# Head of a delta-rule attention and GELU layer kernel: chunks 2 and 3 loaded early, unread products among the row steps, one back turn as ScalarE copies

## The chip, the cores and the metric

The kernel runs on one core of one Trainium2 chip. The metric is the device time of one execution in microseconds, as the median of several runs. One further execution was taken by the hardware profiler, and all views below come from it.

## The reference

Two layers run one after the other. The first is a delta-rule attention with 4 batches, 8 heads, 768 tokens and a head dimension of 48; the second is a layer of 384 -> 2048 -> 384 with an exact GELU over the 3072 tokens that come out of the first.

```
k_n = k / (norm(k) + 1e-6)
for t in range(768):
    y[:, :, t] = q_t @ state
    v_old      = state^T k_n_t
    state      = state + beta_t * outer(k_n_t, v_t - v_old)
x = y.transpose(0, 2, 1, 3).reshape(3072, 384)
h = x @ w_in;  g = 0.5 * h * (1 + erf(h / sqrt(2)));  out = g @ w_out
```

`q`, `k`, `v` and `beta` are 32-bit floats. `w_in` and `w_out` are 64-bit floats: the kernel reads them as pairs of 32-bit words and makes 32-bit floats of them with integer and float operations.

## The kernel before

**Units and chunks.** The 768 tokens are cut into 12 chunks of 64. A unit is one chunk of one pair of batches (one batch in partitions 0 to 63, the other in 64 to 127), so that each chunk has two units (`a` = 0, 1). `first` are the four units of chunks 0 and 1, `third` those of chunk 2, `fourth` those of chunk 3. Two chunks form a group of 32 small triangular systems, which are solved together.

**The head**, the part that the change is about, is written out by hand (L1201 to L1299) in a fixed order on all engines and on the DMA queue SP. In it:

- K and Q of the units are turned on TensorE (`transposed`, L405, part 0 is K and part 1 is Q) and copied out by ScalarE; `grams` (L445) multiplies K by K, `queries` (L463) K by Q.
- `eliminate_steps(0)` (L491) yields the steps that invert the 32x32 triangles of group 0: `scales`, `flip`, thirty row steps `eliminate(j)`, j = 1 to 30 (L528 a product into `tmp`, L530 an addition into `Nu`, both on VectorE), `diagonal`, then three back turns `back(0)` to `back(2)`. A back turn is a VectorE transpose of the whole `Nu`: the first into `XM` (L539), the second into the right half of `Zf`, the third into the left half (both L543). `clear` then sets the lower rows of the left half to zero, mostly on GpSimd (L560).
- `join` (L568) makes the 64x64 inverse of two 32x32 ones at two levels: products on TensorE (`psJ`, L578), at level 0 a VectorE product into `XM` (L589), at level 1 a copy into `Zf` (L593).
- `solve` (`psU`, L792), `use` and `read` (`psY`, L822), `update` (`psS`, L834) and `turn` (`psX`, `xT`, L883) take the two units of chunk 0 to the input of the second layer.

**The weights** come in 16 parts: parts 0 to 7 are `w_in`, 8 to 15 are `w_out`. `fetch(n)` (L234) loads part n from the queue SP, `begin` (L252, or L255 where there is one kink), `exponents` (L258, ScalarE), `mantissas` (L272, L274) and `signed` (L281, L282) decode it. Parts for which `two_kinks(n)` holds have two ScalarE operations in `exponents` and no L281 in `signed`; the others have one ScalarE operation and L281. There are four raw buffers for `w_in`, so that `signed(n)` issues `fetch(n + 4)`, which waits for the last reader of the raw words of part n: L281, or L274 where there is no L281.

**The rest** is a list of steps with due times (`at(first, last, steps)`, from L1316), sorted by time and traced in that order. VectorE and GpSimd run them in just this order; for TensorE, ScalarE and SP a planner takes, at each moment of its own model, the earliest traced instruction that it thinks ready. Instructions that are given to `keep` stay in the traced order on ScalarE. `fc1` (L915) makes the hidden layer of chunks 0 and 1 (16 blocks `f` for each, two to a part of `w_in`), with a GELU into `G` after each block, `fc2` (L933) the output. `load(3)` has 12 DMA issues, `load_v(2)` 4. The tile `G` holds the GELU's results and is idle in the head.

```
def fetch_in(dst, src, u, queues=(nc.sync, nc.sync)):
    ...
    for p in range(2):
        queues[p].dma_start(out=dst[HALF[p]],
```

Of the kernel before, what the change touches and what calls it, by code (L numbers as in the profile page):

```python
# [19 lines left out]
def kernel(  # L20
# [28 lines left out]
    nc = tc.nc  # L49
# [136 lines left out]
    G = Gp[0]  # L186
    spare = Gp[1].rearrange("q a f n -> q (a f n)")
# [51 lines left out]
    def two_kinks(n):  # L239

        return 2 < n < n_in or n_in + 3 < n < n_in + 7
# [27 lines left out]
    def mantissas(n):  # L269
        dst, lo, hi, e = halves[n]  # L270
        bits = dst.bitcast(U32)
        nc.vector.tensor_scalar(bits, hi, 0xFFFFF, 0x100000, op0=ALU.bitwise_and,  # L272
                                op1=ALU.bitwise_or)
        nc.vector.scalar_tensor_tensor(dst, lo, 2.0 ** -32, bits, ALU.mult, ALU.add)  # L274
# [24 lines left out]
    def decode_in():  # L299

        marks = {3: (None, 1.05, 0.99, 1.06), 4: (1.0, 1.09, 1.1, 1.13),
                 5: (1.12, 1.18, 1.14, 1.2), 6: (1.19, 1.24, 1.21, 1.25),
                 7: (1.245, 1.3, 1.29, 1.36)}
        steps = []
        for n, (a, b, c, d) in marks.items():
            if a is not None:
                steps += [(a, (begin, n))]
            steps += [(b, (exponents, n, keep)), (c, (mantissas, n)), (d, (signed, n))]
        return steps
# [95 lines left out]
    def transposed(u, part=(0, 1)):  # L405
        for x in part:
# [10 lines left out]
            flat = (Qp[2 + u.a] if u.c == 3 and x == 0 else (u.Kp, u.Qp)[x]).rearrange("q h d -> q (h d)")  # L417
# [73 lines left out]
    def eliminate_steps(g):  # L491
# [44 lines left out]
        def back(x):  # L536
            nu = Nus[g]
            if x == 0:
                nc.vector.transpose(XMs[g].rearrange("q u c -> q c u"),  # L539
                                    nu.rearrange("q i c -> q c i"))  # L540
            elif x == 1 or g == 0:
                cols = slice(HB, C) if x == 1 else slice(0, HB)
                nc.vector.transpose(Zf[g % 2][:, :, cols].rearrange("q u i -> q i u"), nu)  # L543
            else:
                for p in range(2):
                    top = slice(p * C, p * C + HB)
                    if g > 2:
                        nc.gpsimd.tensor_copy(Zf[0][top, :, 0:HB], Zf[0][top, :, HB:C])
                    else:
                        nc.scalar.copy(Zf[0][top, :, 0:HB], Zf[0][top, :, HB:C])  # L550

        def clear(g):
                for cc in range(2):
                    for p in range(2):
                        part = Zf[g % 2][p * C + HB:(p + 1) * C,
                                         cc * NU // 2:(cc + 1) * NU // 2, 0:HB]
                        if g == cc == p == 0:
                            nc.scalar.mul(part, low[0:HB, 0:HB // 2], 0.0)
                        else:
                            nc.gpsimd.memset(part, 0.0)  # L560

# [3 lines left out]
        steps += [(1.9, back, x) for x in range(3)]  # L565
        return steps + [(0.0, clear, 0)] if g == 0 else steps
# [342 lines left out]
    def fc1(c, f):  # L909
# [8 lines left out]
        if c == 0 or f < EARLY:  # L918
            keep(nc.scalar.activation, *gelu)
        else:  # L920
            nc.scalar.activation(*gelu)  # L921
# [270 lines left out]
    def signs(c0, c1):  # L1192
# [11 lines left out]
        mybir.EngineType.PE, mybir.EngineType.SP}))  # L1204
    load_v(0)
    for n in range(2):
        fetch(n)
    load_k(2, "Kp")
# [13 lines left out]
    scales_, flip_, *rows, back0, back1, back2, clear_ = [s_[1:] for s_ in eliminate_steps(0)]  # L1222
    factors(gms[0], beta_m[:, 0:2].rearrange("q c a h -> q (c a) h"), n0)
    scales_[0]()
    flip_[0]()
# [3 lines left out]
    signs(2, NC)  # L1229
    third = [tiles[2, a] for a in range(NA)]  # L1230
    sums_ = [(u, h) for u in third for h in range(H)]
    for u in first:
        transposed(u, (1,))
        if u.c == 1:
            for x in sums_[5 * u.a:5 * u.a + 5]:
                sum_of_squares(*x)
        queries([u])
    for a in range(NA):
        fetch_q(tiles[2, a])
    for a in range(NA):  # L1240
        fetch_in(Qp[2 + a][:, :, 0:D], k, tiles[3, a])
    for n in range(2, NS):
        fetch(n)
    for n in range(n_in, n_in + 3):
        fetch(n)
    load_v(1)
    for u in third:
        transposed(u, (0,))
    for x in sums_[10:13]:
        sum_of_squares(*x)  # L1250
    grams(third)
    for u in third:
        transposed(u, (1,))
    for x in sums_[13:]:
        sum_of_squares(*x)
    fourth = [tiles[3, a] for a in range(NA)]
    for u in fourth:
        transposed(u, (0,))
    grams(fourth)
    for fn, *args in rows:  # L1260
        fn(*args)
    nc.vector.scalar_tensor_tensor(ng, gms[0][:, 0:NA], -1.0, ns[0], ALU.mult, ALU.mult)
    back0[0](*back0[1:])
    against_state(first[:NA])
    for u in first:
        masked(u)
    back1[0](*back1[1:])
    for a in range(NA):
        join(0, (a,), 0)
    back2[0](*back2[1:])  # L1270
    for a in range(NA):
        join(0, (a,), 1)
    clear_[0](*clear_[1:])
    for u in first[NA:]:
        scale_v(u)
    begin(0)
    exponents(0)
    mantissas(0)
# [30 lines left out]
    def state_at(c, *times, first=(), second=(), last=()):  # L1309

        steps = state_steps(c, first, second, last)
        if len(times) > len(steps):
# [8 lines left out]
             [(t, (join, 0, range(NA, 2 * NA), level)) for level, t in enumerate((1.085, 1.16))],  # L1321
# [24 lines left out]
    plan += [at(2.22, 2.44, [(1.0, scale_head, tiles[c, a], h)  # L1346
# [125 lines left out]
```

## Time and profile before

| quantity | value |
| --- | --- |
| median of 3 runs | 626.86 us (626.41 to 626.89) |
| the profiled execution | 626.5 us, span 624.7 us |
| mean granted TensorE clock | 0.985 |
| TensorE matmul busy | 604.7 us (97%) |
| VectorE busy | 440.4 us (70%) |
| ScalarE busy | 240.5 us (39%) |
| GpSimd busy | 212.8 us (34%) |
| chain that ended last | TensorE 88%, VectorE 5%, ScalarE 3%, DMA 2%, issue 1% |

The span runs from the first to the last instruction; 1.8 us of the profiled execution lie outside it. In the 40 slices of the page, TensorE is busy for 6 to 8 tenths in the first three slices (15.6 us each) and for 9 tenths in nearly all that follow; the granted clock reads 9, 9, 7, 6 in the first four slices and 9 after them. VectorE is busy for 7 to 9 tenths in the first nine slices. A TensorE product of 32-bit floats counts as two instructions (the 64 products of each `fc2` chunk pair are listed as 128), a transpose as one.

### The profile page before, as it was taken

How to read it: one execution, taken by the hardware profiler on the slowest of the kernel's cores; microseconds unless marked ns; L12 is line 12 of the kernel's file. 1: busy time of each engine (PE TensorE's matmuls, PEld its weight loads, DVE VectorE, ACT ScalarE, POOL GpSimd, SP SyncE). 2: the span in 40 equal slices, each digit the busy share in tenths (PEclk: the TensorE clock that was granted, in tenths of full speed). 3: DMA queues.
4: the chain of work that ended last, by engine and by line, in shares of the span. 5: the costliest groups of instructions: out<-in, count | busy, mean ns of one | idle time of the engine just before them, and what ended most of it. 6: DMA issues, size and time to landing. Idle time of an engine off the chain costs nothing.

```text
span 624.7 us, 19703 instructions
## 1 busy us (share of the span) xinstructions
PE 604.7 (97%) x8358; PEld 539.8 (86%) x8358; DVE 440.4 (70%) x811; ACT 240.5 (39%) x546; POOL 212.8 (34%) x316
## 2 busy tenths in 40 slices
PE   6789999999999999999999999999999999999997
PEld 5578786676799999998899998899998899988997
DVE  7999899988967697774859755859745947332532
ACT  3576876265443165224451134451134222044200
POOL 4045002000369821687222885222885200000000
PEclk9976999999999999999999999999999999999999
DMA  9686775101433452353123533013421001010011
GB/s 130 162 269 164 168 185 136 25 1 37 72 41 50 76 92 39 56 115 39 16 44 54 92 73 38 13 31 55 75 50 17 12 3 27 4 24 1 0 27 26
DMA packets 159576, 39.64 MB, mean 63 GB/s; under 512 B 151168, under 2 KB 154368, under 8 KB 159488
## 3 DMA queue, kind: packets, MB, share of 16 engines
q1 hardware_dynamic: 156816, 37.34, 30.7%
q10 hardware_dynamic: 2672, 1.03, 0.8%
q8 instruction: 66, 1.08, 0.7%
q14 instruction: 22, 0.18, 0.1%
HBM read 33.62 MB, written 4.72 MB: 61 GB/s over the span
## 4 chain that ended last, share of the span: by engine, by line
PE 88%; DVE 5%; ACT 3%; DMA 2%; issue 1%; SPq 0%; ACTq 0%
PE psX L966 13%; PE psY L1032 11%; PE psY L966 9%; PE psX L1032 8%; PE psZ L1032 6%; PE psV L1032 6%; PE psH L915 5%; PE psO L933 4%; PE psZ L966 4%; PE psV L966 4%; PE psG L440 3%; PE psK L732 3%; PE psY L822 2%; PE psU L792 2%; PE psQ L752 2%; PE psT L419 2%
## 5 line engine op out<-in xcount | busy, mean ns | idle before, releaser
L377 POOL TENSOR_TENSOR n<-n,half 128x16 f32<-128x16 f32 x10 | 30.8, 3079 | 178.8 <-DVE n L375 131.0
L530 POOL TENSOR_TENSOR Nu<-Nu,tmp 128x30 f32<-128x30 f32 (+14 forms) x120 | 65.3, 544 | 9.4
L528 POOL TENSOR_TENSOR tmp<-Nu 128x30 f32<-128x30 f32 (+14 forms) x120 | 62.5, 520 | 9.4
L1032 PE MATMUL psX<-xT,w_in_sb 128*128 128x256 f32 (+1 forms) x288 | 62.6, 346 | 0.0
L966 PE MATMUL psX<-w_out_sb,G 128*128 128x192 f32 x320 | 56.1, 329 | 0.0
L966 PEld LDWEIGHTS psX<-w_out_sb,G 128*128 128x128 f32 x320 | 52.2, 190 | 0.7
L1032 PEld LDWEIGHTS psX<-xT,w_in_sb 128*128 128x128 f32 x288 | 47.9, 190 | 5.4
L915 PE MATMUL psH<-xT,w_in_sb 128*128 128x256 f32 x192 | 44.6, 386 | 2.3 <-ACT G L921 1.1
L915 PEld LDWEIGHTS psH<-xT,w_in_sb 128*128 128x128 f32 x192 | 36.0, 191 | 9.6 <-ACT G L1015 2.5
L933 PE MATMUL psO<-w_out_sb,G 128*128 128x384 f32 x128 | 43.9, 490 | 0.0
L851 DVE TENSOR_TENSOR V<-psY,y 64x192 f32<-64x192 f32 (+1 forms) x60 | 21.3, 356 | 30.4 <-PE psY L834 26.4
L1060 DVE TENSOR_TENSOR psY<-psY,pu 128x512 f32<-128x512 f32 x20 | 14.0, 700 | 40.3 <-PE psY L1032 40.3
L1032 PE MATMUL psY<-xT,w_in_sb 128*128 128x256 f32 (+1 forms) x192 | 41.5, 345 | 0.0
L1015 ACT COPY xT<-psX 128x768 f32<-128x768 f32 x9 | 7.2, 800 | 79.8 <-PE psX L892 79.8
L1015 ACT COPY pu<-psZ 128x512 f32<-128x512 f32 x40 | 23.5, 587 | 37.5 <-PE psZ L1032 35.0
L933 PEld LDWEIGHTS psO<-w_out_sb,G 128*128 128x128 f32 x128 | 23.5, 190 | 14.2 <-issue 0.3
L1032 PEld LDWEIGHTS psY<-xT,w_in_sb 128*128 128x128 f32 x192 | 32.1, 191 | 3.5
L1015 ACT ACTIVATE G<-G 128x512 f32<-128x512 f32 x40 | 25.2, 631 | 21.2 <-DVE G L1068 21.0
L1068 DVE TENSOR_TENSOR G<-psY,pu 128x512 f32<-128x512 f32 x20 | 13.8, 690 | 22.2 <-PE psY L1032 21.5
L1015 ACT ACTIVATE G<-psY 128x512 f32<-128x512 f32 x20 | 11.9, 596 | 45.2 <-PE psY L1032 45.2
L966 PE MATMUL psY<-w_out_sb,G 128*128 128x192 f32 x160 | 28.1, 329 | 0.0
L966 PE MATMUL psZ<-T,pu 128*128 128x192 f32 x160 | 28.1, 329 | 0.0
(208 smaller groups left out, 1376.2 us busy)
## 6 DMA issues: line engine op xcount, KB each, us to landing
Kp<-in_k_dram SPq DMA_DIRECT2D x76, 96.0 KB, 3.2
w_out_sb<-in_moe_w_in_dram SPq DMA_DIRECT2D x24, 256.0 KB, 4.4
V<-in_v_dram SPq DMA_DIRECT2D x48, 96.0 KB, 3.1
w_raw<-in_moe_w_out_dram SPq DMA_DIRECT2D x12, 384.0 KB, 4.4
out_dram<-o_sb SPq DMA_DIRECT2D x40, 96.0 KB, 2.2
Qp<-in_k_dram SPq DMA_DIRECT2D x64, 32.0 KB, 2.2
G<-in_moe_w_out_dram SPq DMA_DIRECT2D x4, 384.0 KB, 5.1
Qp<-in_q_dram SPq DMA_DIRECT2D x96, 16.0 KB, 2.0
```

Source lines behind the costliest of these rows:

```text
L377: nc.gpsimd.tensor_tensor(flat, flat, half, op=ALU.pow)
L440: nc.tensor.matmul(psG[HALF[p], r, i * NP + j, :], lhsT=u.Kt[rows, p, j, :], rhs=(u.Qt if x else u.Kt)[rows, p, j, :], start=True, stop=True)
L528: rows_on.tensor_tensor(tmp, nu[:, j + 1:, j:j + 1].to_broadcast([128, n, j]), nu[:, j:j + 1, 0:j].to_broadcast([128, n, j]), op=ALU.mult)
L530: rows_on.tensor_tensor(nu[:, j + 1:, 0:j], nu[:, j + 1:, 0:j], tmp, op=ALU.add)
L732: nc.tensor.matmul(u.psK[HALF[p], r, j, :], lhsT=u.Kt[rows, p, j, :], rhs=SQ[rows, u.a, p ^ r, j, 0:w], start=True, stop=True)
L851: nc.vector.tensor_tensor(dst, src, pairs(u.y[at_], s), op=ALU.add)
L915: nc.tensor.matmul(psH, lhsT=w_in_sb[:, f // 2, m, f % 2 * 128:(f % 2 + 1) * 128], rhs=xTs[c][:, m, :], start=(m == 0), stop=(m == NM - 1))
L933: nc.tensor.matmul(u.psO, lhsT=G[:, u.a, f, :], rhs=w_out_sb[:, f, :], start=(f == 0), stop=(f == NF - 1))
L966: nc.tensor.matmul(ps_, lhsT=lhs[:, f, :], rhs=rhs[:, f, :], start=first and f == 0, stop=f == FH - 1, skip_group_check=not first)
L1015: i = fn(*args, **kw)
L1032: nc.tensor.matmul(ps_[:, i], lhsT=lhs[:, f // 2, f % 2 * 128:(f % 2 + 1) * 128], rhs=rhs, start=first and i == 0, stop=True, skip_group_c ...
L1060: nc.vector.tensor_tensor(L1["Y1"], L1["Y1"], L1["pu"][:, 0], op=ALU.add)
```

## The change

What it does, by parts:

1. `Q` of chunk 2 and `K` of chunk 3 get places in the tile `G` (`early_q`, `early_k`, their padding set to zero by four more GpSimd memsets), and their loads, with `K` of chunk 2, are issued ahead of `load_v(0)` and of the first weights. `load_v(1)` and `fetch(2)`, `fetch(3)` follow directly.
2. The turns and products of chunks 2 and 3 (`turned`, `grams`) move from before the row steps to between them: each is tied by a wait to the row step that was traced last (`behind_rows`). Between the others come 59 products of 128 columns that nobody reads (`unread`): 43 behind rows 13 to 30, 10 behind the last row and 6 behind the joins of level 0.
3. The third back turn goes. The left half of `Zf` is filled by ScalarE copies of the right half (`upper_left`), for chunk 0 in the head and for chunk 1 later; its lower rows are set to zero early by two GpSimd memsets.
4. `begin(0)` and half of `mantissas(0)` stand between the joins of level 1, and the second of these is copied out by VectorE. Part 2 of `w_in` becomes one with two kinks.
5. `fetch` of parts 8, 9 and 10 leaves the head for time 1.1, behind `load(3)`, `load_v(2)` and `signed(3)`, whose time goes from 1.06 to 1.081.
6. All GELUs of `fc1` are kept in order on ScalarE, and `scale_head` of chunks 2 and 3 moves from 2.22 to 2.125.

```
+    early_q, early_k = [[G[:, a, 4 * i:4 * i + 4].rearrange("q f (e n) -> q (f e) n", n=C)
+                         for a in range(NA)] for i in range(2)]
+    for a in range(NA):
+        tiles[2, a].Qp = early_q[a]
+        for x in (early_q, early_k):
+            nc.gpsimd.memset(x[a][:, :, D:], 0.0)
...
-        return 2 < n < n_in or n_in + 3 < n < n_in + 7
+        return 1 < n < n_in or n_in + 3 < n < n_in + 7
...
-        marks = {3: (None, 1.05, 0.99, 1.06), 4: (1.0, 1.09, 1.1, 1.13),
+        marks = {3: (None, 1.08, 0.99, 1.081), 4: (1.0, 1.112, 1.1, 1.13),
...
-            elif x == 1 or g == 0:
-                cols = slice(HB, C) if x == 1 else slice(0, HB)
-                nc.vector.transpose(Zf[g % 2][:, :, cols].rearrange("q u i -> q i u"), nu)
+            elif x == 1:
+                nc.vector.transpose(Zf[g % 2][:, :, HB:C].rearrange("q u i -> q i u"), nu)
...
+    def upper_left(us, put=lambda fn, *args: fn(*args)):
+
+        for p in range(2):
+            top = slice(p * C, p * C + HB)
+            put(nc.scalar.copy, Zf[0][top, us, 0:HB], Zf[0][top, us, HB:C])
...
-        if c == 0 or f < EARLY:
-            keep(nc.scalar.activation, *gelu)
-        else:
-            nc.scalar.activation(*gelu)
+        keep(nc.scalar.activation, *gelu)
...
+    load_k(2, "Kp")
+    for a in range(NA):
+        fetch_q(tiles[2, a])
+    for a in range(NA):
+        fetch_in(early_k[a][:, :, 0:D], k, tiles[3, a])
     load_v(0)
     for n in range(2):
         fetch(n)
-    load_k(2, "Kp")
+    load_v(1)
+    for n in range(2, NS):
+        fetch(n)
...
     scales_[0]()
+    for p in range(2):
+        nc.gpsimd.memset(Zf[0][p * C + HB:(p + 1) * C, :, 0:HB], 0.0)
     flip_[0]()
...
+    def behind_rows(fn, *args):
+
+        after = latest(mybir.EngineType.DVE)
+        n = len(nc.cur_bb.bb.instructions)
+        fn(*args)
+        new = next(i for i in nc.cur_bb.bb.instructions[n:] if i.engine == mybir.EngineType.PE)
+        tc.add_manual_dep(new, after.name,
+                          mybir.DependencyInfo(mybir.DependencyClass.Sync,
+                                               mybir.DependencyReason.DATA), reason="time")
+
+    def unread(*cols):
+
+        psI = ps.tile([128, 512], F32, tag="mlp", name="psI")
+        for n in cols:
+            nc.tensor.matmul(psI[:, 0:n], lhsT=ident,
+                             rhs=Kp[0].rearrange("q h d -> q (h d)")[:, 0:n], start=True, stop=True)
...
+    between = {12: [(turned, third, 0)], 13: [(unread, *[128] * 5)], 14: [(grams, third)],
+               15: [(turned, third, 1)], 16: [(unread, *[128] * 5)], 17: [(turned, fourth, 0)],
+               18: [(unread, *[128] * 4)], 19: [(grams, fourth)]}
+    between.update({j: [(unread, *[128] * 3)] for j in range(20, 26)})
+    between.update({j: [(unread, 128, 128)] for j in range(26, HB - 1)})
+    between[25] = [(unread, *[128] * 4)]
     for fn, *args in rows:
         fn(*args)
+        for step in between.get(args[0], ()) if args else ():
+            behind_rows(*step)
...
     nc.vector.scalar_tensor_tensor(ng, gms[0][:, 0:NA], -1.0, ns[0], ALU.mult, ALU.mult)
+    behind_rows(unread, *[128] * 10)
     back0[0](*back0[1:])
-    against_state(first[:NA])
-    for u in first:
+    against_state(first[:1])
+    for u in first[:3]:
         masked(u)
+    against_state(first[1:NA])
+    masked(first[3])
     back1[0](*back1[1:])
+    upper_left(slice(0, NA * H))
     for a in range(NA):
         join(0, (a,), 0)
-    back2[0](*back2[1:])
-    for a in range(NA):
-        join(0, (a,), 1)
-    clear_[0](*clear_[1:])
+    unread(*[128] * 6)
+    begin(0)
+    join(0, (0,), 1)
+    exponents(0)
+    mantissas(0, (0,))
+    join(0, (1,), 1, nc.vector.tensor_copy)
+    mantissas(0, (1,))
     for u in first[NA:]:
         scale_v(u)
-    begin(0)
-    exponents(0)
-    mantissas(0)
...
+             at(1.05, 1.051, [(1.0, upper_left, slice(NA * H, NU), keep)]),
+             at(1.1, 1.102, [(1.0, fetch, n_in + i) for i in range(3)]),
...
-    plan += [at(2.22, 2.44, [(1.0, scale_head, tiles[c, a], h)
+    plan += [at(2.125, 2.35, [(1.0, scale_head, tiles[c, a], h)
```

## The prediction

> **What bounds the kernel now.** I read the busy times by stretches first, then the chain of waits, then the timelines of VectorE and of the queue SP. From 67 us on TensorE hardly pauses, so the end moves as far as the work ahead of it does. In the chain, VectorE carries the head: rows, back turns, joins, decoding.
>
> The stretches (us, busy time and instructions of PE, PEld, DVE, ACT, POOL; then the granted clock):
>
> ```profile
> 36.00:37.00 1.00, 0.69 (x5) 0.45 (x3) 0.91 (x3) 0.96 (x3) 0.00 (x0) 1.00 0.79 264
> 37.00:38.00 1.00, 0.00 (x0) 0.00 (x0) 0.89 (x4) 0.98 (x2) 0.00 (x0) 1.00 0.68 176
> 39.00:40.00 1.00, 0.38 (x7) 0.14 (x5) 1.00 (x3) 1.00 (x7) 0.89 (x2) 0.80 0.95 330
> 40.00:41.00 1.00, 1.00 (x37) 1.00 (x40) 1.00 (x1) 0.41 (x1) 1.00 (x2) 0.50 1.02 269
> 56.00:57.00 1.00, 1.00 (x7) 0.87 (x4) 1.00 (x2) 0.40 (x1) 1.00 (x1) 0.66 0.06 16
> ```
>
> After a nearly idle stretch on TensorE the clock halves near 39.6 (0.80 in that stretch), and it comes back only at 56.7, when the first full products of the layer run; VectorE stands at 0.9 to 1.0 throughout. VectorE's timeline:
>
> ```profile
> 44.27 0.86 DVE L589 TENSOR_TENSOR XM<-psJ,gm 32x256 f32<-32x256 f32 x2 [0.39 <-PE psJ L578]
> 45.16 1.93 DVE L543 STREAM_TRANSPOSE Zf<-Nu 128x1024 f32<-128x1024 f32 x1
> 46.93 0.55 DVE L255 TENSOR_SCALAR w_e<-w_out_sb 128x768 uint32<-128x768 uint32 x1
> 47.39 0.97 DVE L272 TENSOR_SCALAR w_in_sb<-w_out_sb 128x768 uint32<-128x768 uint32 x1
> 52.19 1.47 DVE L282 SCALAR_TENSOR_TENSOR w_in_sb<-w_in_sb,w_e 128x768 f32<-128x768 f32 x1
> 53.69 1.07 DVE L255 TENSOR_SCALAR w_e<-w_out_sb 128x768 uint32<-128x768 uint32 x1
> 59.07 0.95 DVE L281 SCALAR_TENSOR_TENSOR w_e<-w_out_sb,w_e 128x768 uint32<-128x768 uint32 x1
> 77.28 1.02 DVE L765 TENSOR_TENSOR V<-psK,V 128x384 f32<-128x384 f32 x2 [0.75 <-ACT y L756]
> ```
>
> The third back turn, the wait of 0.39 ahead of the joins and three operations longer than their like (0.97, 1.47 and 1.07 against 0.55, 0.96 and 0.55) are in line. The queue SP (start, us to issue):
>
> ```profile
> 52.18 9.15 SPq L234 DMA_DIRECT2D w_out_sb<-in_moe_w_in_dram  x9
> 61.46 1.28 SPq L100 DMA_DIRECT2D Kp<-in_k_dram  x2
> 62.98 2.44 SPq L234 DMA_DIRECT2D w_out_sb<-in_moe_w_in_dram  x3
> 65.47 2.59 SPq L119 DMA_DIRECT2D Qp<-in_q_dram  x4
> 68.17 1.28 SPq L100 DMA_DIRECT2D Kp<-in_k_dram  x2
> 69.50 2.62 SPq L119 DMA_DIRECT2D Qp<-in_q_dram  x4
> 72.22 3.35 SPq L100 DMA_DIRECT2D V<-in_v_dram  x4
> ```
>
> SP issues without a break from 61.5 to 76: two K loads of `load(3)`, then part 7 of `w_in` as soon as its buffer is free (62.98), then the rest of `load(3)` and `load_v(2)`. The earliest traced ready DMA goes first.
>
> **Part by part**, against the profiled 626.5 us (span 624.7 and 1.8 outside; 0.36 under the median, to which I add the result).
>
> Early loads: 4 K, 8 Q and 4 K issues move ahead of V and weights. At their rates now (3.98, 7.26, 2.65 us) they end near 26; V of chunk 0 follows to 30, parts 0 and 1 to 33, V of chunk 1 to 38, parts 2 and 3 to 42. With some 5 us to land, V is there by 34 (wanted 39.1), part 0 by 38 (wanted 45), part 2 by 46 (wanted 54). K of chunk 3 lands near 29 for row 17 at 29.1; late, it would hold only TensorE. Cost nothing; the cover is 5 us.
>
> Row steps: they stay at 0.22 to 0.41 us each on VectorE and end at 38.9. Two memsets of 32x1024 on GpSimd now lie at 16 to 19 beside them. The row of such a memset beside L272 shows 0.42 lost, beside the following L274 (two inputs, 0.96) nothing; I take 0, with 0.4 as the far end. [...]
>
> Unread products: 59, two instructions each. The same shape, `psX` L879, runs two in 0.22 us, so 13 us of TensorE in time that waits for rows. The ten behind row 30 take 2.2 us and end at 41.2, just when the first back turn delivers `XM`. At half clock it is 4.4 us. I take the full clock, since no gap over 0.5 us is left between rows 12 and 30; the other end is a rival.
>
> VectorE, 43 to `begin(3)` at 60.94: third turn -1.93; wait for `psJ` -0.39, since the products of chunk 3 no longer stand ahead; L281 of part 2 -0.95; two copies of 32x256 +0.85 (as L589). The stretched operations of now (1.45) go, but `begin(0)` at 44.7 meets GpSimd's `masked` (39.1 + 0.81 + 3 x 1.24 + 0.81 + 1.24 = 45.7, +0.97), and `mantissas(0)` meets `scale_v`, which no longer waits for V (+0.8): 1.77 in place of 1.45. Sum -2.1; bounds -3.0 (half the contention) and -1.2.
>
> TensorE to the first `psH` at 56.01: `Zf` of the second unit is copied out at 48.35; `psU` 0.6, three copies 1.0, `psY` 0.7, then ScalarE's six copies of `x`, `xT`, 0.94 of `exponents(1)` and `xT` end near 53.9. So -2.0. Later a re-halved clock would add 1 us here, but the second joins still wait for L589 of VectorE near 64.
>
> ScalarE: 2.5 us of `upper_left`, one Prelu more (1.17), less 1.4 of copies; it lies in waits for `psH` (0.9 to 1.9 us each now). `scale_head` starts earlier, yet 20 heads of 0.24 now precede the GELU of block 8 where 7 did: 117.2 + 4.8 + two output copies 1.0 + two issue pairs 2.3 = 125.3, against 125.29. Nothing; bounds -1.1 (the wait of `psH` there) and +0.3.
>
> Now the queue. `fetch(7)` is traced at 1.081, behind the 12 issues of `load(3)` (1.0625) and the 4 of `load_v(2)` (1.0705). SP comes free after parts 5 and 6: L281 of part 1 ends at 57.1 - 1.1 = 56.0 (-1.93 - 0.39 + 0.85 + 0.32), plus 6 x 0.43 = 58.6. Sixteen issues (1.28 + 2.59 + 1.28 + 2.62 + 3.35 = 11.1) end at 69.7; the third of part 7 starts at 70.6 and lands 4.5 us later (as now) at 75.1. VectorE would reach `begin(7)` at 73.64 - 2.1 = 71.5: **a new wait of 3.6 us**, and queued behind it are `signed(6)`, all `w_out` parts and whoever wants them. From there VectorE needs 2.9 + 1.9 + 0.95 to the end of part 7: 80.9, after 80.1 now (the 0.75 at L765 is gone). TensorE wants part 7 at 82.8 now, at 80.8 with its 2.0: it loses 0.4. At the next need (`w_out` part 1, ready at 90.16 now, when TensorE arrives at 90.33) VectorE stands where it was (+0.85 less 0.88 of waits for `psY` at 86.8 and 87.7), so TensorE must fill 1.4 us with the turns of chunk 1 or its first blocks. The planner does that now at 100.7 (`psH` between two `psO`). Parts 8 to 10 add 6 issues behind part 7, landing from 76 for `begin(8)` near 80. From 104.9 on TensorE is never short of decoded weights.
>
> Sum: -2.0 at the first `psH`, +0.4 at part 7: **-1.6, that is 625.3 us**; with the bounds of contention and filling -2.5 to -0.2.
>
> **Rivals.**
> - Part 7 in time: the planner's model holds `load(3)` back, or takes the weights first, as at 62.98. Then the -2.1 of VectorE goes through, and with half the contention -3.0: 624.3. For it: only two loads went ahead so far; against: part 7 was then traced first.
> - Nothing left: no filling at `w_out` parts 1 to 3, so TensorE ends where VectorE does, -0.2: 626.6. For it: 90.16 stands so near 90.33.
> - Slower by the queue: part 7 lands later still, at 7.1 us after issue (the longest landing of these loads), with an extra wait of SP: `begin(7)` near 79. It decides from 77.1, since 5.7 us later is 82.8, when TensorE wants part 7 now. At 79 it is +1.9: 628.7.
> - The clock falls nevertheless: ten products take 4.4 us, the joins 1.1 each and six products 2.6, so the copy of the second join ends at 51 instead of 48.35, part 7 follows +2.7, end +2.5: 629.3. Against it: the fall at 39.6 came after 2.9 us, less than half of them busy, and no such stretch is left. [...]
>
> **Chances.** Forecast 0.40, part 7 in time 0.27, nothing left 0.18, queue 0.10, clock 0.05. 0.2% is 1.25 us, about what a measurement can tell from no change. Faster by that: 0.28 of the 0.40 and 0.26 of the 0.27, with 0.01: 0.55. Slower: the last two and 0.01, 0.16. Same: 0.29. The range 623.3 to 627.9 takes in the forecast, the first two rivals with their bounds, and the nearer half of the third; the forecast's own is 624.4 to 626.7.
>
> **What would show it.** Right: granted clock 1.0 from 36 to 45; `begin(3)` near 58.8; first `psH` near 54; on SP sixteen loads ahead of part 7 and `begin(7)` waiting some 3.6 us for it; L765 without a wait; the `psH` wait of 1.1 near 125 still there. Wrong: clock 0.5 at 41 (head), part 7 issued ahead of Q of chunk 3 (queue), `psO` standing still at 90 to 98 (no filling), or a GELU of block 8 before 124 (ScalarE).

## The result and the profile after

The change makes the kernel **slower: 634.84 us** (median of four, 634.44 to 636.62) against 626.63 us of the kernel before on the same chip (626.34 to 626.89). The ratio is 1.0137, 95% interval 1.0116 to 1.0157, or +8.2 us where -1.6 was forecast. The profiled execution of after took 636.62 us (span 634.9), the longest of the four, and its times are compared with the profiled 626.5 of before.

The stretches (columns as before the change: PE, PEld, DVE, ACT, POOL, granted clock, DMA share, GB/s):

```profile
40.00:41.00 1.00, 1.00 (x12) 1.00 (x11) 1.00 (x1) 0.72 (x7) 1.00 (x2) 1.00 0.78 252
47.00:48.00 1.00, 1.00 (x16) 0.88 (x15) 0.95 (x3) 0.00 (x0) 1.00 (x2) 1.00 0.00 0
79.00:80.00 1.00, 0.00 (x0) 0.00 (x0) 0.00 (x0) 0.00 (x0) 0.00 (x0) 1.00 0.96 338
80.00:81.00 1.00, 0.00 (x0) 0.00 (x0) 0.00 (x0) 0.00 (x0) 0.00 (x0) 0.96 1.01 387
81.00:82.00 1.00, 0.00 (x0) 0.00 (x0) 0.66 (x2) 0.06 (x1) 0.00 (x0) 0.50 1.01 406
90.00:91.00 1.00, 1.00 (x22) 0.49 (x20) 0.97 (x2) 1.00 (x2) 0.00 (x0) 0.50 0.05 11
91.00:92.00 1.00, 1.00 (x57) 0.95 (x54) 1.00 (x2) 0.01 (x1) 0.00 (x0) 0.92 0.36 49
```

The fall near 40 is gone, as the unread products were to bring about. A new one has come at 81, after two stretches in which no engine but the DMA does anything, and it lasts until 91. TensorE's timeline shows what leads up to both places:

```profile
33.24 1.16 PE L427 MATMUL psT<-ident,G 128*128 128x128 f32 x8 [1.82 <-ACT SQ L428]
36.31 8.97 PE L1264 MATMUL psI<-Kp,ident 128*128 128x128 f32 x78
45.22 1.20 PE L580 MATMUL psJ<-XM,G 32*32 32x32 f32 x64
85.09 5.49 PE L917 MATMUL psH<-xT,w_in_sb 128*128 128x256 f32 x12 [6.40 <-ACT G L1014]
132.81 1.56 PE L917 MATMUL psH<-xT,w_in_sb 128*128 128x256 f32 x6 [0.46 <-ACT o_sb L936]
135.97 8.04 PE L917 MATMUL psH<-xT,w_in_sb 128*128 128x256 f32 x36 [1.59 <-ACT G L1014]
```

`XM` is there at 41.2, but the first joins begin at 45.22, behind 78 instructions of unread products. At 85 TensorE has stood for 6.40 us, and its next 12 instructions take 5.49 us where 12 such take 2.86 at the full clock. At 136 it is 10.26 us behind the kernel before (125.71); 10.1 us is the whole difference of the two profiled executions, so nothing is lost later. The timeline of the queue SP in after, from the end of part 6's issues on:

```profile
60.60 1.28 SPq L100 DMA_DIRECT2D Kp<-in_k_dram  x2
61.93 2.61 SPq L119 DMA_DIRECT2D Qp<-in_q_dram  x4
64.98 2.56 SPq L100 DMA_DIRECT2D Kp<-in_k_dram  x2
67.59 2.62 SPq L119 DMA_DIRECT2D Qp<-in_q_dram  x4
70.33 3.71 SPq L100 DMA_DIRECT2D V<-in_v_dram  x4
74.13 1.52 SPq L240 DMA_DIRECT2D w_out_sb<-in_moe_w_in_dram  x3
75.69 3.67 SPq L240 DMA_DIRECT2D w_raw<-in_moe_w_out_dram  x6
```

VectorE's timeline in after, at the joins, at `begin(3)` and at `begin(7)`:

```profile
45.96 1.75 DVE L591 TENSOR_TENSOR XM<-psJ,gm 32x256 f32<-32x256 f32 x4 [2.83 <-PE psJ L580]
60.60 0.56 DVE L258 TENSOR_SCALAR w_e<-w_out_sb 128x768 int32<-128x768 int32 x1
81.34 0.56 DVE L258 TENSOR_SCALAR w_e<-w_out_sb 128x768 int32<-128x768 int32 x1 [8.12 <-DMA w_out_sb<-in_moe_w_in_dram]
81.82 0.95 DVE L290 SCALAR_TENSOR_TENSOR w_in_sb<-w_in_sb,w_e 128x768 f32<-128x768 f32 x1
```

And ScalarE's timeline in after, behind `begin(7)`:

```profile
81.94 2.12 ACT L1014 ACTIVATE w_e<-w_e,lim 128x768 f32<-128x768 int32 x2 [7.62 <-DVE w_e L258]
84.65 0.67 ACT L1014 ACTIVATE G<-psH 128x256 f32<-128x256 f32 x2
```

Read together: sixteen issues stand ahead of part 7 on SP, `begin(7)` waits 8.12 us for its words, ScalarE waits 7.62 us with `exponents(7)`, which is kept in order, and two GELUs whose products are long done (84.65) wait behind that. So `psH` gets no free buffer, TensorE stops at 78.7, and the clock falls (0.50 from 81). Part 6 is late as well: `signed(6)` (L290 at 81.82) stands directly behind `begin(7)` on VectorE, and the two blocks that TensorE wants at 78.7 need part 6, which is ready at 82.77. Of the 6.40 us, 4.1 would be lost with free buffers too, and the last 2.3 are due to the GELUs.

### The profile page after: what moved, and what is told of

Its sections match the earlier page's. It is cut to its first block, busy times and chain, and to the rows that moved or that the text cites. A ratio compares the mean times of both kernels' runs of the same rounds, so it can differ in the third digit from the quotient of the medians.

```text
span 634.9 us, 19968 instructions
## 1 busy us (share of the span) xinstructions
PE 611.7 (96%) x8476; PEld 545.9 (86%) x8476; DVE 436.5 (69%) x811; ACT 242.8 (38%) x548; POOL 212.3 (33%) x319
## 3 DMA queue, kind: packets, MB, share of 16 engines
q10 hardware_dynamic: 2672, 1.03, 0.8%
## 4 chain that ended last, share of the span: by engine, by line
PE 88%; DVE 3%; DMA 2%; ACT 2%; SPq 2%; issue 1%; ACTq 0%; DVEq 0%
PE psX L965 13%; PE psY L1031 11%; PE psY L965 8%; PE psX L1031 8%; PE psV L1031 6%; PE psZ L1031 6%; PE psO L932 4%; PE psZ L965 4%; PE psV L965 4%; PE psH L917 4%; PE psG L448 3%; PE psK L734 3%; PE psI L1264 2%; PE psY L824 2%; DMA w_out_sb<-in_moe_w_in_dram 2%; PE psU L794 2%
## 5 line engine op out<-in xcount | busy, mean ns | idle before, releaser
L917 PE MATMUL psH<-xT,w_in_sb 128*128 128x256 f32 x192 | 47.9, 402 | 9.9 <-ACT G L1014 9.0
L1014 ACT ACTIVATE G<-psY 128x512 f32<-128x512 f32 x20 | 11.9, 596 | 45.2 <-PE psY L1031 45.2
L965 PE MATMUL psY<-T,G 128*128 128x192 f32 x160 | 28.0, 329 | 0.0
```

Source lines behind the costliest of these rows:

```text
L917: nc.tensor.matmul(psH, lhsT=w_in_sb[:, f // 2, m, f % 2 * 128:(f % 2 + 1) * 128], rhs=xTs[c][:, m, :], start=(m == 0), stop=(m == NM - 1))
L965: nc.tensor.matmul(ps_, lhsT=lhs[:, f, :], rhs=rhs[:, f, :], start=first and f == 0, stop=f == FH - 1, skip_group_check=not first)
L1014: i = fn(*args, **kw)
```

## The experiments

Theory: the loss is part 7 behind sixteen issues and what follows from it. Rivals: the unread products hold up the joins; ScalarE's new order; `w_out` fetched later. Each median stands beside runs of the kernel before on the same chip (626.8 to 627.2 in these sessions), each interval is 95%.

### Four runs on the queue

**1. Queue mended.** In the change, `load(3)` and `load_v(2)` go behind `signed(3)`:

```
-    plan += [at(1.06, 1.065, [(1.0, load, 3)]),
+    plan += [at(1.09, 1.095, [(1.0, load, 3)]),
...
-    plan += [..., at(1.07, 1.071, [(1.0, load_v, 2)]), ...]
+    plan += [..., at(1.096, 1.097, [(1.0, load_v, 2)]), ...]
```

> The change with one thing altered: the loads of load(3) and load_v(2) are due behind signed(3), so that part 7 stands behind two of these issues instead of sixteen. Theory (the queue: part 7 late, then a starved TensorE and its halved clock): part 7 is issued near 62 and lands before VectorE wants it at 73.2, the wait of 8.1 us and the clock of 0.50 from 81 to 91 go, and the time is that of before less 0.3 at begin(3) plus about 1 of ScalarE near 130: 626 to 628 us. Rival (the head: the unread products hold up the joins): the head stays as it is, so 633 or more. Rival (ScalarE: kept GELUs, scale_head earlier): 633 or more.

631.56 us (629.9 to 636.74), ratio 1.0089 (1.0054 to 1.0125). Part 7 is no longer waited for, but some 4.8 us over before remain. The profiled execution is one of two long ones (635.7): TensorE is slow up to 31 us in it (below), and all that follows is 5 us later. VectorE now waits for parts 8 and 9 (its waits: us, times, longest):

```profile
DVE w_e L261 <- DMA w_raw<-in_moe_w_out_dram: 3.1, 2, 2.3
```

TensorE stands behind their exponents (its timeline):

```profile
88.81 1.56 PE L917 MATMUL psH<-xT,w_in_sb 128*128 128x256 f32 x6 [1.39 <-ACT G L1014]
91.73 1.56 PE L917 MATMUL psH<-xT,w_in_sb 128*128 128x256 f32 x6 [1.36 <-ACT G L1014]
```

**2. No unread products**, by a line in `behind_rows`.

```
+        if fn is unread:
+            return
...
-    unread(*[128] * 6)
```

> The change without its 59 unread products. Queue theory: part 7 still stands behind sixteen issues, so 632 to 636 us; the clock falls near 40 as before, the joins of level 0 begin near 41.5 instead of 45.2 at half the clock. Rival (the head): the time goes back by what the joins lose, 2 to 3 us or more, and to 627 if this was the whole loss.

632.85 us (632.01 to 634.96), 1.0101 (1.0080 to 1.0123), as the queue theory has it. This run tells most about the prediction: without unread products `begin(3)` comes at 58.80, where 58.8 was forecast, and part 7 is waited for by 3.64 us, where 3.6 was (VectorE's timeline):

```profile
76.86 0.56 DVE L258 TENSOR_SCALAR w_e<-w_out_sb 128x768 int32<-128x768 int32 x1 [3.64 <-DMA w_out_sb<-in_moe_w_in_dram]
```

TensorE's timeline right behind it:

```profile
80.61 4.54 PE L917 MATMUL psH<-xT,w_in_sb 128*128 128x256 f32 x12 [1.92 <-DVE V L767]
```

Even so TensorE loses 3.9 us here: ahead of it, it is 0.5 us earlier than before (a `psH` at 75.83 after 76.35), behind it 3.4 us later (next `psU` at 85.08 after 81.72). It stands for 1.92 us, and its next 12 instructions take 4.54 us at the halved clock. The forecast had 0.4. Here `signed(6)` ends at 78.29, before TensorE wants it, so only the buffers hold TensorE up. The profile names VectorE's L767 as what ended the wait. The first GELU ends at the same moment (80.56), and by the code it is the GELU that frees the buffer these blocks take; both stand behind `exponents(7)`.

**3. Both** (`behind_issue` holds an issue behind the last one traced on SP, for `load(3)` as below, and likewise for `load_v(2)` and parts 8 to 11; no unread products).

```
-    plan += [at(1.06, 1.065, [(1.0, load, 3)]),
+    plan += [at(1.09, 1.095, [(1.0, behind_issue, load, 3)]),
```

> Both: part 7 ahead of load(3), load_v(2) and parts 8 to 10, and no unread product. Against the run with the queue alone mended: if the unread products as placed cost more than the clock that they hold is worth, this is faster by 1 to 2 us (625 to 626); if the held clock is worth more, it is slower by 1 to 2 us (628 to 629); VectorE's begin(3) tells the same, 60.6 with them, below 59.5 or above 61.5 without.

630.56 us (629.35 to 630.91), 1.0050 (1.0035 to 1.0065): one us under the run with them; the intervals overlap.

**4. The queue's fault alone, in the kernel before.**

```
-        marks = {3: (None, 1.05, 0.99, 1.06), ...
+        marks = {3: (None, 1.08, 0.99, 1.081), ...
```

> The kernel before with only the mark of part 3 altered as in the change (exponents at 1.08, signed at 1.081), so that part 7 is queued behind the sixteen issues of load(3) and load_v(2); nothing else of the change. Queue theory: issued at 61.5 + 13.4 = 74.9, landed near 81, VectorE waits 7 us at begin(7) (73.64 before), TensorE starves and its clock falls: 632 to 635 us, as much as the whole change loses. Rivals (head, ScalarE): at most 1 or 2 us over before, under 629.

634.05 us (631.34 to 634.8), 1.0101 (1.0077 to 1.0126). The two later marks of part 3 alone make most of the loss, and the wait for part 7 is there again (VectorE's timeline):

```profile
81.38 0.56 DVE L252 TENSOR_SCALAR w_e<-w_out_sb 128x768 int32<-128x768 int32 x1 [6.80 <-DMA w_out_sb<-in_moe_w_in_dram]
```

and TensorE's:

```profile
85.13 5.09 PE L915 MATMUL psH<-xT,w_in_sb 128*128 128x256 f32 x12 [5.08 <-DVE V L765]
```

TensorE stops at 80.05 here. Of the loss in this execution, 0.8 us came ahead of the wait (first `psH` at 56.78 after 56.01). As in run 2, the profile names VectorE's reader of `psK`, which ends together with the first GELU (85.08).

### Four runs on what is left

**5. Queue mended, parts 8 to 10 fetched in the head again** (behind part 3; the line at 1.1 goes).

```
+    for n in range(n_in, n_in + 3):
+        fetch(n)
     new_group(0)
...
-             at(1.1, 1.102, [(1.0, fetch, n_in + i) for i in range(3)]),
```

> The run with the queue mended for part 7, and parts 8 to 10 of w_out fetched in the head again, as before. That run still lost 3.8 us. Theory (three further places: begin of parts 8 and 9 late, since their six issues came behind load(3) and load_v(2), with the GELUs kept behind their exponents; ScalarE near 130; the head): the waits of VectorE for the raw words of parts 8 and 9 (2.3 and 0.8 us) and those of psH for the GELU near 85 (1.4 and 1.4) go, 2.4 us less: 628 us (627.3 to 628.7). Rival (all that is left is in the head): 630 or more as it was.

630.74 us (628.13 to 632.74), 1.0060 (1.0040 to 1.0079). The waits for parts 8 and 9 and the two of 1.4 us are gone, but the time falls by 0.8 us only in the medians, 1.8 by the ratios, and the intervals overlap. Something came in their place: at 44 to 48 the DMA share is 1.02 again (0.02 in after), and TensorE waits at `psU` for nothing that the profile shows ("issue"), 0.44 and then 1.38 us; with the loads later, 0.44 alone. Behind these waits the granted clock falls (0.56 over 52 to 56, 0.58 over 56 to 60, 1.00 ahead of them), and the first `psH` is at 58.50 after 56.17 in after. TensorE's timeline of this run:

```profile
49.30 0.44 PE L794 MATMUL psU<-V,Zf 64*64 64x48 f32 x14 [0.44 <-issue]
51.12 0.97 PE L794 MATMUL psU<-V,Zf 64*64 64x48 f32 x50 [1.38 <-issue]
```

**6. And ScalarE as before** (the old rule of which GELUs are kept, `scale_head` at 2.22).

```
-        keep(nc.scalar.activation, *gelu)
+        (keep only if c == 0 or f < EARLY)
-    plan += [at(2.125, 2.35, [(1.0, scale_head, ...
+    plan += [at(2.22, 2.44, [(1.0, scale_head, ...
```

> The same, and part 6 of the change undone (GELUs kept only for chunk 0 and the first blocks of chunk 1, scale_head at 2.22). If the two waits of psH near 130 (0.46 for o_sb and 1.59 for the GELU, where before one of 1.13 stood) are ScalarE's order, another 0.9 to 1.2 us go: 626.8 us, the time of before, since the head as a whole is even (first psH 56.17 after 56.01). If they are not, the same as the run without it.

629.06 us (626.73 to 632.23), 1.0033 (1.0014 to 1.0052). The wait for `o_sb` is gone and that for the GELU is 1.13 again: ScalarE's part is 1.2 us in the trace.

**7. And no unread products.**

```
+        if fn is unread:
+            return
...
-    unread(*[128] * 6)
```

> The same without the 59 unread products: the clock falls near 40 and the joins run at half of it, but nothing stands ahead of them. Queue mended without them gave 630.6 against 631.6 with them. Theory (as placed, the unread products cost TensorE as much as the clock that they hold is worth): within 1 us of the run with them, and first psH near 55.3. Rival (the held clock is worth the 2 us of the prediction): slower by 1.5 to 2 us.

626.88 us (624.68 to 628.97), 0.9998 (0.9984 to 1.0011), the time of before. So the unread products cost 2.2 us as placed. The trace without them shows where VectorE's gain goes: `begin(3)` is at 59.38, but `exponents(3)` (due 1.08, behind the copies of `upper_left`) comes at 61.62 after 61.53 before. VectorE's timeline, at the end of part 3:

```profile
63.77 0.96 DVE L290 SCALAR_TENSOR_TENSOR w_in_sb<-w_in_sb,w_e 128x768 f32<-128x768 f32 x1 [1.91 <-ACT w_e L1017]
```

**8. As 6, with 22 fewer unread products** (none behind rows 20 to 25, 8 behind the last row, 4 behind the joins).

```
-    between.update({j: [(unread, *[128] * 3)] for j in range(20, 26)})
-    between[25] = [(unread, *[128] * 4)]
-    behind_rows(unread, *[128] * 10)
+    behind_rows(unread, *[128] * 8)
...
-    unread(*[128] * 6)
+    unread(*[128] * 4)
```

> The same with 22 fewer unread products: none behind rows 20 to 25, 8 instead of 10 behind the last row, 4 instead of 6 behind the joins of level 0, so that TensorE, which is 5 us behind the rows at 36, is done when XM comes at 41.2. Theory (the prediction's mechanism was right, its count of TensorE's work wrong): the clock stays at 1.0, the joins of level 0 begin near 41.5 instead of 45.2, first psH near 54 and the time 624.5 to 625.5. Rival (the gain of the head is given back later, at w_out parts 1 to 3): 626 to 626.8 although the first psH comes 2 us earlier. Rival (the clock falls with fewer of them): 626.5 to 628 and a clock of 0.5 in the joins.

628.20 us (626.58 to 630.34), 1.0019 (1.0007 to 1.0031): joins at 46.26 in the profiled execution, no gain that the intervals show. This execution is the longest of its twelve (630.34), and TensorE ran slowly until 34 in it (its timeline, then the stretch):

```profile
25.93 1.13 PE L448 MATMUL psG<-Qt,Kt 48*64 48x64 f32 x32
```
```profile
24.00:28.00 4.00, 4.00 (x78) 3.43 (x77) 3.69 (x10) 2.28 (x4) 0.00 (x0) 1.00 0.82 147
```

The same 32 products take 0.69 us in after at 24.00. The granted clock reads 1.00 in both.

### Four runs on the slow start

Seven unread products of `ident` by `ident` go to the very start of TensorE's order, where it waits for the first K.

```
+    for _ in range(7):
+        nc.tensor.matmul(psI[:, 0:128], lhsT=ident, rhs=ident, start=True, stop=True)
```

**9 to 12**: onto run 7, run 6, run 8, and the kernel before.

> In all traces so far the same instructions of TensorE take 1.6 times as long in the first 22 to 35 us (32 products of psG 1.13 us, later 0.69) although the granted clock reads 1.00 there; the executions in which the quick rate comes at 22.7 are the shorter ones. This is the run without unread products (queue, w_out and ScalarE put right), with seven products of ident by ident that nobody reads put at the very start, 1.5 to 4.6 us, where TensorE waits for the first K. Theory (the rate comes from work done without a break, and sets how far TensorE lags): the quick rate comes before 10 us, the row steps begin up to 0.5 us earlier, but with no filler the clock still falls near 34: 626.0 to 626.9. Rival (the slow rate is the chip's own start and not to be moved): no change of any duration, 626.9.

> The run with all 59 unread products (queue, w_out and ScalarE put right), with the seven products at the start. If its spread of 626.7 to 632.2 is that of the moment at which the quick rate comes, the slow executions go and it stands at 626.7 to 628, still with the joins of level 0 near 45, since the unread products behind the rows last 8.97 us from 36.3 even at the quick rate. Rival (the spread has another cause): median 629 as it was.

> The run with 22 fewer unread products (628.2, its two shortest 626.6 and 626.8), with the seven products at the start. If TensorE is quick from the start, it is done with the rows' work when XM comes, joins near 41.5, first psH near 54: 624.5 to 626. If the gain of the head is given back later: 626.5 to 627 with joins near 41.5. If the start does not hold the rate: 628.

> The kernel before with the seven products at the start and nothing else. TensorE is not what its head waits for until the joins near 42, where its clock is 0.50: within 0.5 us of 626.8 by the theory; by the rival that the early rate carries the head, 1 us or more less.

628.68 (1.0031, 1.0019 to 1.0042), 629.63 (1.0040, 1.0027 to 1.0053), 628.16 (1.0016, 1.0003 to 1.0030) and 629.66 us (1.0039, 1.0026 to 1.0052): all four forecasts missed, and the kernel before itself loses 2.7 us by 14 instructions. The quick rate does come early (four transposes take 0.63 to 0.64 us instead of 1.1, from 4.7 us on in runs 9 and 11, from 6.2 in runs 10 and 12), so in these runs work moves the slow start. But TensorE then stands in `psD` for 2.40 us ("issue") in run 12 where it stood for 0.25, so that it goes on when it did before: as if its instructions were not there yet. The wait is behind the same number of its products (220 in before and in run 12), and so 14 of them earlier in the program. Behind it the products run at the slow rate again (32 of `psG` in 1.14 us at 21 to 31 in run 12, 0.69 in after), and the mean granted clock of run 12 is 0.965 after 0.985. With 14 more instructions ahead the later waits of this kind lie elsewhere too, in the kernel before at the last of the 64 instructions of the second joins (TensorE's timeline of run 12):

```profile
48.29 0.20 PE L578 MATMUL psJ<-Zf,XM 32*32 32x32 f32 x1 [2.03 <-issue]
```

### Six runs towards a better version

**13. As 6, with 23 unread products**: 5 behind row 16, 2 behind each of rows 26 to 30, 4 behind the last, 4 behind the joins.

```
-    between = {12: [(turned, third, 0)], 13: [(unread, *[128] * 5)], 14: [(grams, third)],
+    between = {12: [(turned, third, 0)], 14: [(grams, third)],
...
-               18: [(unread, *[128] * 4)], 19: [(grams, fourth)]}
-    between.update({j: [(unread, *[128] * 3)] for j in range(20, 26)})
+               19: [(grams, fourth)]}
...
-    between[25] = [(unread, *[128] * 4)]
...
-    behind_rows(unread, *[128] * 10)
+    behind_rows(unread, *[128] * 4)
...
-    unread(*[128] * 6)
+    unread(*[128] * 4)
```

> Queue, w_out and ScalarE put right as in the run that took 629.1 with all 59 unread products and 626.9 with none; here 23: 5 behind row 16 (ahead of the stall of 1.8 us for ScalarE), 2 behind each of rows 26 to 30, 4 behind the last row, 4 behind the joins of level 0. Theory (the unread products cost because TensorE gets 4 us behind the rows, not because they are of no use): TensorE is done by 41, the joins of level 0 begin near 41.5 at clock 1.0, first psH near 54: 624.5 to 626. Rival (the head's gain is given back where VectorE waits for the exponents of part 3, 1.9 us at L290 in the run without unread products): joins early, first psH early, and 626.5 to 627.5 all the same.

630.49 us, 1.0049 (1.0034 to 1.0064). The joins begin at 41.32 at the full clock, as the theory wants. Then the copy of the second join, which the change gave to VectorE behind `begin(0)` and half of `mantissas(0)`, holds `psU` up by 1.90 us, an issue wait of 2.30 us follows, the clock falls all the same (three `psX` take 0.90 us behind it, 0.55 in run 6), and the first `psH` is at 57.00. TensorE's timeline:

```profile
41.32 1.20 PE L580 MATMUL psJ<-XM,G 32*32 32x32 f32 x64 [0.47 <-POOL P L482]
48.41 0.68 PE L794 MATMUL psU<-V,Zf 64*64 64x48 f32 x32 [1.90 <-DVE Zf L595]
51.76 1.32 PE L824 MATMUL psY<-V,P 64*64 64x48 f32 x39 [2.30 <-issue]
```

**14. And eight sums of squares moved** behind the turns of chunk 3.

```
-        if args and args[0] in (14, 16, 19):
+        if args and args[0] in (18, 19):   # sums_[:8], then sums_[8:]
```

> The same with the first eight sums of squares on ScalarE moved behind the turns of chunk 3 (row 18), so that they no longer stand ahead of the copies of psT. If the stall of TensorE at 31.4 to 33.2 comes from them, it is at most 0.9 us, TensorE is 0.9 us earlier at 36, and the time is the same or up to 0.5 us less, since at 36 TensorE then waits for the rows. Rival (the stall comes from the four copies of G and diag, 2.3 us): 1.8 us as it was.

630.78 us, 1.0058 (1.0038 to 1.0078). The stall at 31 falls from 1.83 to 0.93, so half of it was the sums. TensorE then waits 2.86 us for row 26, the clock falls, and the 28 unread instructions take 6.29 us instead of 3.80.

**15. And part 3's marks of before**, `upper_left` of chunk 1 behind them.

```
-        marks = {3: (None, 1.08, 0.99, 1.081), ...
+        marks = {3: (None, 1.05, 0.99, 1.06), ...
-             at(1.05, 1.051, [(1.0, upper_left, slice(NA * H, NU), keep)]),
+             at(1.082, 1.0821, [(1.0, upper_left, slice(NA * H, NU), keep)]),
```

> The same with exponents(3) at 1.05 and signed(3) at 1.06 as before and the copies of the upper left part for chunk 1 at 1.082 behind them. If VectorE's gain in the head is lost at L290 of part 3 (waits of 1.9 to 3.1 us in the runs with an earlier head, none in the kernel before), the wait falls to under 0.7 us and the time by 1 us or more below the run with the marks of the change: 624 to 625.5. Rival (TensorE carries from the first psH on, whatever VectorE does): the same time, though the wait is gone.

629.70 us, 1.0038 (1.0023 to 1.0053). The longest wait at L290 falls from 1.3 to 0.3, and the `psH` of block 8 begin at 124.55, 1.16 us ahead of before. Yet the span is 628.9: 5.4 us are lost after that, part of it here (TensorE's timeline):

```profile
318.62 1.16 PE L448 MATMUL psG<-Kt 48*64 48x64 f32 x62
321.50 0.32 PE L448 MATMUL psG<-Kt 48*64 48x64 f32 x2 [1.72 <-issue]
416.91 0.81 PE L448 MATMUL psG<-Kt 48*64 48x64 f32 x40 [1.18 <-issue]
```

The granted clock is 0.96 over 300 to 340 (1.00 from 140 to 300), and the 16 instructions of `psZ` behind the 1.72 us take 4.23 us where 16 such take 2.76 at 348.51, which adds to the loss.

**16. And parts 8 to 10 behind part 7**, ahead of the rest of `load(3)`.

```
+             at(1.083, 1.084, [(1.0, behind_issue, fetch, n_in + i) for i in range(3)]),
```

> The same, but parts 8 to 10 of w_out are fetched not in the head but right behind part 7 and ahead of the rest of load(3) and of load_v(2): part 5 of the change with its order put right. The head's loads of 44 to 48 us (DMA share 1.02) then no longer stand beside the waits of TensorE for instructions at psU (0.4 to 1.4 us). If these waits are due to those loads, 0.5 to 1 us less: 623.5 to 625. If part 7 now lands late with six loads behind it (6 us after issue where they shared, wanted at 72): 0.5 to 2 us more.

628.37 us (626.55 to 632.0), 1.0021 (1.0007 to 1.0035). Part 7 is not waited for. It could not test the issue waits, since with this number of instructions run 15 has none at `psU` either; the intervals overlap.

**17. Run 15 with TensorE's instructions brought to the number of the change**, 8476 instead of 8404, by 36 more unread products behind rows 20 to 25, 26 of them short (16 columns, 32 rows).

```
+    between.update({j: [(fill, 2 if j < 25 else 0, 5 if j < 22 else 4)] for j in range(20, 26)})
```

> The run with 23 unread products and part 3's marks of before had block 8 of the layer at 124.55, 1.2 us ahead of the kernel before, and still a span 4.2 us longer: after 300 us TensorE waits 2.9 us for instructions at psG (issue) in places where the kernel before (8358 TensorE instructions) and the change (8476) do not wait at all; with 8404 instructions these waits come where 64 small products run in 1.2 us. Here 36 more unread products behind rows 20 to 25 (10 of 128 columns, 26 of 16 columns on 32 rows, short) bring TensorE to 8476 as in the change; nothing else. Theory (where the instruction stream is reloaded follows the number of instructions before it): the waits at psG after 300 go, 3 us and more less than that run: 625 to 626.8; the rows' gap of 2.9 us at 34 to 37 is filled as well, so the clock stays at 1.0 up to the joins. Rival (the late waits are chance): 629 to 630 with waits at psG.

**626.83 us** (624.23 to 628.05), 0.9991 (0.9977 to 1.0004): 2.9 us less for more work. The fill also changes the head, but the gain lies behind it: in the profiled execution the `psH` of block 8 begin at 126.47, 1.9 us later than in run 15, and the span is 3.0 us shorter. So the part behind, with the same instructions in both, takes 4.9 us less, of which the issue waits give 2.5 (3.5 to 1.0). After 140 us one issue wait is left, at the same place as in before and after (0.5 in both). TensorE's waits from 140 us on, then its timeline in the head:

```profile
PE psY L836 <- issue: 1.0, 1, 1.0
```
```profile
50.34 1.62 PE L794 MATMUL psU<-V,Zf 64*64 64x48 f32 x49 [3.16 <-issue]
```

With this number the wait in the head falls into `psU` again, beside the loads (DMA share 1.01 at 44 to 48), and takes 3.16 us; the head's gain is lost there.

**18. And the second join copied out before `begin(0)`.**

```
-    begin(0)
     join(0, (0,), 1)
-    exponents(0)
-    mantissas(0, (0,))
     join(0, (1,), 1, nc.vector.tensor_copy)
-    mantissas(0, (1,))
+    begin(0)
+    exponents(0)
+    mantissas(0)
```

> The same, and VectorE copies the second join of level 1 out before it begins part 0, not behind begin(0) and half of its mantissas: in the runs with an earlier head TensorE waited 1.4 to 1.9 us for that copy at the second psU. Theory: that wait falls under 0.7 us, first psH 1 us earlier than in the run beside it, and 0.5 to 1 us less in time: 624 to 626. Rival (VectorE then waits for the second join itself, 1 us, and part 0 comes later by that): the same time, or 0.5 us more.

627.29 us (625.3 to 628.6), 1.0005 (0.9996 to 1.0013). VectorE waits 1.0 us for the join instead, as the rival has it; the first `psH` is 1.2 us earlier, but the issue wait is also shorter (1.72 instead of 3.16), so the run decides nothing. No version measured beats the kernel before. Run 17 with the fetches of run 16, which would take the loads from beside that wait, was not tried.

## Why the prediction was wrong

**The step that failed: the price of the wait at part 7.** The place was right, the wait was forecast, and run 4 shows that part 3's later marks, which bring it about, make 1.0% by themselves. Wrong were its size and, more, who waits for it.

- Size: 8.1 us instead of 3.6. SP came free at 60.6 instead of 58.6; the sixteen issues took 13.4 us instead of 11.1; part 7 landed 6.0 us after its third issue began instead of 4.5, with parts 8 to 10 right behind it. VectorE came 1.7 us later than forecast (73.2), or the wait would have been longer still. The "slower by the queue" rival had the mechanism and the turning point (77.1; it was 81.3), but a chance of 0.10.
- Who waits: the text named `signed(6)`, `w_out` "and whoever wants them", and then let TensorE want only part 7, at 80.8, for a loss of 0.4. ScalarE's kept `exponents(7)` stands ahead of two GELUs that free `psH`. And `signed(6)` behind `begin(7)` keeps back the blocks that TensorE wants next, in after for 4.1 us of its stop. So TensorE stops at 78.7 in the change, with part 7 late by 8.1 us (after) or by 3.6 (run 2). Run 2, with the forecast wait, lost 3.9 us at this place.
- The clock: its fall was priced in the head and forgotten here. Of the 3.9 us of run 2, 1.9 are the pause and 1.7 are 12 instructions at the halved clock (4.54 against 2.86). In run 2 the clock falls at a pause of 1.92 us; in after the pause is 6.40 us, and the clock is at 0.50 for 10.2 us.

**Unread products, "end at 41.2".** Failed: they ended at 45.2. The row groups were added up one by one, but not TensorE's own time for all that stands between them: 1.82 us of stall for ScalarE, then 78 instructions in one line of 8.97 us. The clock held, as forecast, and the joins ran in 1.20 us, but the row of VectorE shows what they cost: 2.83 and 0.43 us of waits for `psJ`, where -0.39 was entered. Runs 6 and 7 put it at 2.2 us. The rival "clock falls nevertheless" had the lag but tied it to the halved clock.

**VectorE, -2.1 by `begin(3)`.** -0.34 in after, and -2.1 (58.80) in run 2: the terms were right, without the unread products. The contention (1.77) did not come in after: `begin(0)` takes 0.56 there, beside GpSimd's `scale_v`. It came without the unread products, in run 2 (L261 takes 1.39 us) and in run 7 (L261 1.41, L279 1.18). What the sum lacked is that the gain ends at `exponents(3)`, whose new mark is part of the change (run 7, 1.91 us; gone in run 15).

**First `psH`, -2.0.** +0.16 in after; in run 2, at the halved clock (the 64 instructions of a join in 1.92 us, 1.20 in after), -0.48.

**Parts 8 to 10, "landing from 76".** Failed: issued 75.7 to 79.4. In after the wait for part 7 hides it; with part 7 mended, 2.75 us of TensorE show (run 1). These waits are nested, so the parts do not add up: by the ratios, the queue's fault costs 6.3 us alone (run 4) and gives back 3.0 when it is mended in the change (run 1).

**ScalarE, "nothing; -1.1 to +0.3".** +1.2: block 8 begins 5.08 us after the pair of blocks before it instead of 3.89, and 3.88 again in run 6. The sum had the right pieces, and lacked the wait of 0.46 for the output copy behind nine heads of `scale_head`.

**Right:** row steps, early loads and memsets cost nothing (rows end at 39.0, 38.9 before). "Nothing left" and "part 7 in time" did not arise.

Of run 17's version, the parts of the change that can be kept cost and gain nothing that these runs can tell. Open is how much of the executions' spread (1 to 7 us among the runs of one changed version, up to 2.6 in before) is the moment at which TensorE becomes quick, and how much the issue waits. That these are TensorE waiting for its instructions, or an instruction stream being reloaded, as run 17's theory has it, is argued from their places, not shown.

## What to carry to other kernels

When a load is moved behind others on a queue, follow its wait through every engine that runs in a fixed order to the last buffer that it keeps from coming free; and where TensorE is at the end of that chain, add what the fallen clock costs afterwards, in run 2 nearly as much as the pause itself (1.7 us beside 1.9). Filler work needs a budget of its own engine: sum everything in its order against the clock time in which the other engine's steps pass, and leave slack. Compare variants at the same number of TensorE instructions, or read the issue waits of the whole run first: with the number changed by 72, and the fill that changed it in the head, the part behind the head took 4.9 us less (run 17).

## What the runs showed of the hardware

- TensorE starts slow, and the granted clock column does not show it: 32 instructions of `psG` take 1.13 to 1.14 us at 21 to 31 in the kernel before, and 0.69 once it is quick (24.00 in after), at 1.00 in the column both times. In after the quick rate comes at 22.7, in run 1, with the same head, near 31; with seven products at the start (14 instructions, 3.2 to 3.4 us) it is there at 4.7 (runs 9 and 11) or 6.2 (runs 10 and 12). The traces have no record of the clock ahead of 36.2 us in before and of 22.9 in after, and the column reads 1.00 there. In before nothing between 5 and 35 us runs at the quick rate, so the fall at 39.6 that the prediction read was only the first that the column shows. Why the quick rate comes only at 22 to 36 us without those products is open: in before TensorE was busy for 4.25 us of 5 to 10 and 4.75 of 10 to 15 without becoming quick.
- TensorE's issue waits were counted in before and after, with all instructions of its queue in the trace (products, weight loads and the rest). They lie behind number 450 (0.25 us in before, 0.27 in after), behind 706 (1.15 in both), and behind 7618 in before and 7874 in after (0.47 in both), within one; these numbers are multiples of 256 apart. Only those directly ahead of the first `psU` (1.57 us in before, 0.44 in after) do not: they go with the place in the program. In run 15 the longest, 1.72 us, stands among 64 short instructions that take 1.2. Number 1986 in after is the 15th instruction of `psU`. There is no wait near it in after and in run 1 (the DMA share at 44 to 48 is 0.02 in after); behind the 14th or 15th there are 1.38, 0.83, 3.16 and 1.72 us in runs 5, 6, 17 and 18, where that share is 1.01 to 1.03. The share is not the only difference between these runs, so that it lengthens the wait is not shown.
- In run 2 the clock halved at a pause of 1.92 us on TensorE ahead of 12 large products: 0.50 from 81, 0.79 over 84 to 85, 1.00 again at 85. The changes of the clock that the traces of before and after record lie 3.41 us apart or a multiple of it (in before at 36.19, 39.61 and 56.67, in after at 22.90, 80.92 and 91.16), and in run 2 the pause makes just over half of the 3.41 us that end at 81.00.
